# Merging two weight matrices as plain f32 products, in an attention and gated-layer kernel on one core

## The chip, the core and the metric

The kernel runs on one core of one Trainium2 chip. The metric is device time in microseconds (us); the times shown are of whole executions, and the profile is one execution recorded by the hardware.

## What is computed

The reference, cut to what matters (shapes: batch 4, 8 heads, 576 positions, head size 64; 2304 tokens of width 512):

```python
scores = scale * np.matmul(q, k.transpose(0, 1, 3, 2))
thresh = np.max(scores, axis=-1, keepdims=True) - tau
scores = np.where(scores >= thresh, scores, -1000000000.0)
...
x = attention output as [2304, 512]
x = (sigmoid(x @ w_gate) * (x @ w_val)) @ w_out        # d_ff 1536
a = x @ w1
b = x @ w2
h = a * b @ w3                                         # w3 is 1024 x 1024
out = h @ w_out2                                       # w_out2 is 1024 x 512
```

Weights arrive as 64-bit floats. Since `(a * b @ w3) @ w_out2` equals `(a * b) @ (w3 @ w_out2)`, the kernel forms the 1024 x 512 product `w3 @ w_out2` itself, once. This is the merge, and it is all that the change touches.

## The kernel before

**Stages.** Attention runs over 16 head pairs (4 batches of 4 pairs), each in 9 steps of 128 query rows, so 144 steps g (36 to a batch, 9 to a pair). A step's scores go into one of two PSUM buffers `ps_s` (`s_mm`, PE), then the row maximum (`s_max`, DVE, L321), the exponential and threshold (`s_exp`, ACT, L327 and L328), the mask into the tile `e` (`s_mask`, DVE, L336), a split of `e` into two f16 halves (`s_hi`, `s_lo`, ACT and POOL in batch 0), a DMA transpose into `pt` (`s_tr`, SP queue, L364), and 5 steps later the product with v (`pv`, PE, into `u`). The scores of step g+2 reuse the buffer of step g, so they wait for the mask of g. The first gated layer (`l1_gen`) of a batch runs beside the attention of the next batch, and that of the last batch after it; it can't begin before the attention of its batch is done (`ready`). The second layer and its output close the kernel (`ps_ab`, `ps_y`).

**A pair's inputs.** q and k are loaded, transposed on PE (`ps_t<-ident,qm` and `ps_t<-ident,km`, L156), split by ACT and DVE into a high and a low part, and copied by DMA into the stacked operands `qa`, `ka` (L206 to L210) and `ylz` (L216) of the scores. The table `ahead` (L826) says at which step of the pair before each of these pieces is issued.

**The merge.** `merge_gen` (L491) is a generator. `ucast` turns a loaded 128 x 512 block of 64-bit weights into f32: two DVE operations (L450, L456), one ACT (L455), one POOL (L459, tile `f`). There are 24 blocks: 8 of `w_out2` (`"o"`), 16 halves of the rows of `w3` (`"r"`). A block of `w_out2` is also split into a high part `woh` (ACT, L468) and a low part `wol` (DVE, L469). `trans` transposes half a row of `w3` with four PE transposes (L530), and splits the result from PSUM into `th` (ACT, L534) and `tl` (DVE, L535). For each of 8 rows, 8 products of 128 x 128 by 128 x 512 follow, each as three matmuls in the reduced format f32r (`three`, L471: high by low, low by high, high by high). The row's result is stored to DRAM as `sc_m` (L568) and is read again only in the last stage (L1114). All 12 first blocks are cast before the first product.

**What sets the order.** The attention loop calls `filler` (L838) twice in each step, which runs the merge for 700 ns of the generator's own prices (L841: `merge = run(merge, 700.0)`), and the first layer once the merge has ended. The scores, maxima, exponentials and masks are issued with a higher priority (L869). A scheduler then fixes the order of each engine's instructions by these priorities and by when it believes them ready, so the written place of a merge product isn't where it stands on PE. Each engine works its own list in order: an instruction that waits holds all behind it. All DMAs are issued from one list, that of SP.

Of the kernel before, what the change touches and what calls it, by code (L numbers as in the profile page):

```python
# [8 lines left out]
F32 = mybir.dt.float32  # L9
# [13 lines left out]
def kernel(  # L23
# [464 lines left out]
    def raw_slot(n):  # L488
        return XR[:, n % KC, 2 * S:2 * S + 2 * UW]

    def merge_gen():  # L491
        woh = mp.tile([P, NF2, DM], F32R, name="woh")
        wol = mp.tile([P, NF2, DM], F32R, name="wol")
        units = [("o", i, 0) for i in range(NF2)] + [("r", 0, 0), ("r", 0, 1)]
        units += [("r", i, h) for i in range(1, NF2) for h in range(2)]
        raws, rows, tr, done = {}, {}, {}, [0]

# [7 lines left out]
        def ucast():  # L505
            n = done[0]
            if n >= len(units):
                return
            done[0] += 1
            uload(n + 3)  # L510
            nm, i, h = units[n]
            t1 = mp.tile([P, UW], U32, tag="t1", name="t1", bufs=2)
            t2 = mp.tile([P, UW], I32, tag="t2", name="t2", bufs=2)
            f = mp.tile([P, UW], I32, tag="f", name="f", bufs=3)
            cast64(f, raws.pop(n), t1, t2)
            if nm == "o":
                split(woh[:, i], wol[:, i], f.bitcast(F32), nc.vector)
            else:
                rows[i, h] = f.bitcast(F32)

        def trans(i, h):
            if h == 0:
                tr[i] = tuple(
                    mp.tile([P, NF2, P], F32R, tag=g, name=g, bufs=2) for g in ("th", "tl")
                )
            th, tl = tr[i]
            r = rows.pop((i, h))
            ps = bank("ps_3")
            for j in range(4):
                nc.tensor.transpose(ps[:, j * P:(j + 1) * P], r[:, j * P:(j + 1) * P], ident)  # L530
            hs = slice(4 * h, 4 * h + 4)

            def out():
                nc.scalar.activation(th[:, hs].rearrange("p a b -> p (a b)"), ps, AF.Copy)  # L534
                nc.vector.tensor_tensor(  # L535
                    tl[:, hs].rearrange("p a b -> p (a b)"), ps,
                    th[:, hs].rearrange("p a b -> p (a b)").bitcast(F32), op=ALU.subtract,
                )

            defer.append(out)  # L540

        for n in range(3):
            uload(n)
        yield 0
        for i in range(NF2 + 4):
            ucast()
            yield 600.0
        trans(0, 0)
        trans(0, 1)
        yield 8 * 110  # L550
        flush(0)
        for i in range(NF2):
            th, tl = tr.pop(i)
            ps = bank("ps_34")
            for kk in range(NF2):
                three(
                    ps, (th[:, kk], tl[:, kk]), (woh[:, kk], wol[:, kk]),
                    kk == 0, kk == NF2 - 1,
                )
                if kk in (1, 4):  # L560
                    ucast()
                if kk in (2, 5) and i + 1 < NF2:
                    trans(i + 1, kk // 3)
                yield T(512, 3) + (4 * 110 if kk in (2, 5) else 0)
            def out(i=i, ps=ps):
                mo = mp.tile([P, DM], F32, tag="mo", name="mo", bufs=2)
                nc.scalar.activation(mo, ps, AF.Copy)
                nc.sync.dma_start(sc_m[i], mo)  # L568

            flush(0)  # L570
            defer.append(out)
        flush(0)


# [263 lines left out]
    def filler(g, half):  # L838
        nonlocal l1, merge, lp, lb
        if merge is not None:  # L840
            merge = run(merge, 700.0)  # L841
            if merge is None:
                mctx.close()
                spent[0] = 0
# [336 lines left out]
```

## Time and profile before

| | |
|---|---|
| Median of 3 executions | 1119.03 us (1117.58 to 1123.13) |
| Span of the profiled execution | 1115.6 us |
| Median less that span | 3.4 us |
| PE busy | 1008.3 us (90%) |
| DVE busy | 774.8 us (69%) |
| POOL busy | 676.3 us (61%) |
| ACT busy | 627.6 us (56%) |

The page gives the profiled execution's own time as its span; what lies around the span is not in it. Busy shares are averages over stages with different limits, so the stage in which the merge runs has to be read by itself: by its windows, by the order in which its steps start, and by what PE did in between. A matmul's record lasts longer than it holds PE, since matmuls are pipelined; how much PE time one costs is read from the distance of two starts.

### The profile page before, as it was taken

How to read it: one execution, taken by the hardware profiler on the slowest of the kernel's cores; microseconds unless marked ns; L12 is line 12 of the kernel's file. 1: busy time of each engine (PE TensorE's matmuls, PEld its weight loads, DVE VectorE, ACT ScalarE, POOL GpSimd, SP SyncE). 2: the span in 40 equal slices, each digit the busy share in tenths (PEclk: the TensorE clock that was granted, in tenths of full speed). 3: DMA queues.
4: the chain of work that ended last, by engine and by line, in shares of the span. 5: the costliest groups of instructions: out<-in, count | busy, mean ns of one | idle time of the engine just before them, and what ended most of it. 6: DMA issues, size and time to landing. Idle time of an engine off the chain costs nothing. (4 is left out here: it accounts for less than half of the span.)

```text
span 1115.6 us, 20323 instructions
## 1 busy us (share of the span) xinstructions
PE 1008.3 (90%) x6960; PEld 884.9 (79%) x6960; DVE 774.8 (69%) x1380; ACT 627.6 (56%) x1245; POOL 676.3 (61%) x577
## 2 busy tenths in 40 slices
PE   2598956898987999999999998999999999999997
PEld 2477845676765787777877888999999989988996
DVE  6978687888897767767877645776767644652741
ACT  4868898767777676567667644554442322331321
POOL 3755475587888586678677855677664643462530
PEclk9789967999988999999999999999999999999999
DMA  8999999999999999898988864677558826844922
GB/s 227 245 274 211 225 218 173 241 280 264 270 286 235 200 209 210 211 210 180 201 198 184 161 140 153 215 234 250 184 193 293 256 80 229 282 131 128 325 69 63
DMA packets 322422, 232.57 MB, mean 208 GB/s; under 512 B 225296, under 2 KB 253968, under 8 KB 322320
## 3 DMA queue, kind: packets, MB, share of 16 engines
q1 hardware_dynamic: 322320, 231.28, 80.9%
q8 instruction: 55, 0.90, 0.3%
q14 instruction: 47, 0.39, 0.1%
HBM read 133.17 MB, written 30.93 MB: 147 GB/s over the span
## 5 line engine op out<-in xcount | busy, mean ns | idle before, releaser
L358 POOL TENSOR_TENSOR h<-e,h 128x576 f16<-128x576 f32 x90 | 120.1, 1336 | 39.9 <-ACT e L355 29.7
L327 ACT ACTIVATE e<-ps_s,nm 128x576 f32<-128x576 f32 x144 | 106.1, 737 | 51.0 <-DVE nm L321 49.8
L336 DVE SCALAR_TENSOR_TENSOR e<-ps_s,th,e 128x576 f32<-128x576 f32 x144 | 116.2, 811 | 20.3 <-ACT th L328 12.5
L63 PEld LDWEIGHTS <-pt 128*128 128x128 f16 x2240 | 82.1, 101 | 58.8 <-DMA pt<-h 32.3
L321 DVE TENSOR_REDUCE nm<-ps_s 128x1 f32<-128x576 f32 x144 | 106.3, 751 | 28.9 <-PE ps_s L63 19.9
L344 ACT ACTIVATE h<-e 128x576 f16<-128x576 f32 x144 | 97.0, 678 | 28.3 <-DVE e L336 14.8
L63 PE MATMUL ps_s<-ka,qa 128*128 128x288 f32 x256 | 67.5, 351 | 42.2 <-DVE e L336 31.4
L63 PE MATMUL ps_h<-xl,gh 128*128 128x512 f32 (+1 forms) x240 | 94.7, 395 | 6.3 <-POOL xl L469 2.8
L63 PE MATMUL ps_h<-xl,vh 128*128 128x512 f32 (+1 forms) x240 | 92.7, 386 | 2.4 <-ACT th L685 1.3
L63 PE MATMUL ps_h<-xh,gl 128*128 128x512 f32 (+1 forms) x240 | 91.3, 380 | 3.3 <-POOL gl L469 3.3
L469 POOL TENSOR_TENSOR gl<-wg,gh 128x512 fp32r<-128x512 f32 x42 | 55.4, 1319 | 61.4 <-ACT gh L468 61.4
L63 PE MATMUL ps_y<-wm,abh 128*128 128x512 f32 x288 | 91.6, 390 | 0.2 <-DVE wm L469 0.2
L63 PE MATMUL ps_h<-xh,vl 128*128 128x512 f32 (+1 forms) x240 | 90.2, 376 | 1.6 <-POOL vl L469 1.6
L63 PE MATMUL ps_o<-gvl,oh 128*128 128x512 f32 (+1 forms) x240 | 90.4, 376 | 1.0 <-DVE XR L718 1.0
L63 PE MATMUL ps_h<-xh,gh 128*128 128x512 f32 (+1 forms) x240 | 90.8, 378 | 0.0
L63 PE MATMUL ps_h<-xh,vh 128*128 128x512 f32 (+1 forms) x240 | 90.2, 376 | 0.0
L63 PE MATMUL ps_o<-gvh,ol 128*128 128x512 f32 (+1 forms) x240 | 88.5, 369 | 0.3 <-POOL ol L469 0.3
L63 PE MATMUL ps_o<-gvh,oh 128*128 128x512 f32 (+1 forms) x240 | 88.2, 368 | 0.0
L63 PE MATMUL u<-vh,pt 128*128 128x64 f16 x640 | 62.6, 200 | 27.6 <-DMA pt<-h 27.2
L63 PEld LDWEIGHTS ps_s<-ka,qa 128*128 128x128 f32 x256 | 45.6, 210 | 50.5 <-DVE e L336 36.5
L360 DVE SCALAR_TENSOR_TENSOR h<-e,h 128x576 f16<-128x576 f32 x54 | 61.4, 1137 | 23.2 <-ACT h L344 22.8
L469 POOL TENSOR_TENSOR ol<-wo,oh 128x512 fp32r<-128x512 f32 x42 | 55.7, 1330 | 24.0 <-ACT oh L468 23.9
(198 smaller groups left out, 3025.2 us busy)
## 6 DMA issues: line engine op xcount, KB each, us to landing
wc<-sc_c SPq DMA_DIRECT2D x168, 256.0 KB, 3.2
sc_c<-wc SPq DMA_DIRECT2D x56, 256.0 KB, 2.9
XR<-in_moe_w_out_dram SPq DMA_DIRECT2D x20, 512.0 KB, 5.0
ka<-xk SPq DMA_DIRECT2D x64, 144.0 KB, 3.3
wg<-sc_g SPq DMA_DIRECT2D x36, 256.0 KB, 3.1
wv<-sc_v SPq DMA_DIRECT2D x36, 256.0 KB, 3.1
wo<-sc_o SPq DMA_DIRECT2D x36, 256.0 KB, 3.2
XR<-in_moe_w_dram SPq DMA_DIRECT2D x16, 512.0 KB, 5.0
```

What stands on the lines that cost most here:

```text
L63: nc.tensor.matmul(out_, lhsT, rhs, start=first, stop=last)
L321: nc.vector.tensor_reduce(nm, x["ps"], axis=AX.X, op=ALU.max, negate=True)
L327: nc.scalar.activation(e, x["ps"], AF.Exp, bias=x["nm"])
L336: nc.vector.scalar_tensor_tensor(x["e"], x["ps"], x["th"], x["e"], op0=ALU.is_ge, op1=ALU.mult, accum_out=prep[pr]["sum"][:, s:s + 1],)
L344: nc.scalar.activation(x["h16"][:, 0:S], x["e"], AF.Copy, scale=PSC)
L358: nc.gpsimd.tensor_tensor(lo, e, hi, op=ALU.subtract)
L360: nc.vector.scalar_tensor_tensor(lo, e, PSC, hi, op0=ALU.mult, op1=ALU.subtract)
L469: (lo_eng or nc.gpsimd).tensor_tensor(lo, x, hi.bitcast(F32), op=ALU.subtract)
```

## The change

The merge's products take unsplit f32 operands: one plain f32 matmul each (L564 of the changed kernel) instead of three f32r ones. `woh`, `wol`, `th` and `tl` go; `wo` and `wt` (one f32 tile each) stand in their place, the cast writes straight into `wo`, and `trans` leaves one ACT copy. The first half row of `w3` is cast first, then four blocks of `w_out2`, the other half, and the other four; the products of the first row begin after three casts and are issued between the rest. `filler` gives the merge, in each call, its remaining price divided by the calls that are left in batch 0.

```diff
+    CAST_NS = 600.0
+    MERGE_NS = NF2 * (NF2 * T(512, 4) + 8 * 110) + (NF2 + 4) * CAST_NS
+
     def merge_gen():
-        woh = mp.tile([P, NF2, DM], F32R, name="woh")
-        wol = mp.tile([P, NF2, DM], F32R, name="wol")
-        units = [("o", i, 0) for i in range(NF2)] + [("r", 0, 0), ("r", 0, 1)]
+        wo = mp.tile([P, NF2, DM], I32, name="wo")
+        units = [("r", 0, 0)] + [("o", i, 0) for i in range(NF2 // 2)]
+        units += [("r", 0, 1)] + [("o", i, 0) for i in range(NF2 // 2, NF2)]
         units += [("r", i, h) for i in range(1, NF2) for h in range(2)]
...
-            f = mp.tile([P, UW], I32, tag="f", name="f", bufs=3)
-            cast64(f, raws.pop(n), t1, t2)
             if nm == "o":
-                split(woh[:, i], wol[:, i], f.bitcast(F32), nc.vector)
+                cast64(wo[:, i], raws.pop(n), t1, t2)
             else:
+                f = mp.tile([P, UW], I32, tag="f", name="f", bufs=4)
+                cast64(f, raws.pop(n), t1, t2)
                 rows[i, h] = f.bitcast(F32)
...
-            def out():
-                nc.scalar.activation(th[:, hs].rearrange("p a b -> p (a b)"), ps, AF.Copy)
-                nc.vector.tensor_tensor(
-                    tl[:, hs].rearrange("p a b -> p (a b)"), ps,
-                    th[:, hs].rearrange("p a b -> p (a b)").bitcast(F32), op=ALU.subtract,
+            defer.append(
+                lambda: nc.scalar.activation(
+                    t[:, hs].rearrange("p a b -> p (a b)"), ps, AF.Copy
                 )
-
-            defer.append(out)
+            )
...
-        for i in range(NF2 + 4):
+        for n in range(3):
             ucast()
-            yield 600.0
+            yield CAST_NS
         trans(0, 0)
-        trans(0, 1)
-        yield 8 * 110
+        yield 4 * 110
...
             for kk in range(NF2):
-                three(
-                    ps, (th[:, kk], tl[:, kk]), (woh[:, kk], wol[:, kk]),
-                    kk == 0, kk == NF2 - 1,
-                )
-                if kk in (1, 4):
+                ns = T(512, 4)
+                if i == 0:
+                    for _ in range(2 if kk == 6 else 1):
+                        ucast()
+                        ns += CAST_NS
+                    if kk == 4:
+                        flush(0)
+                    if kk == 3:
+                        trans(0, 1)
+                        ns += 4 * 110
+                elif kk in (1, 4):
                     ucast()
+                mm(ps, t[:, kk], wo[:, kk].bitcast(F32), kk == 0, kk == NF2 - 1)
...
-            merge = run(merge, 700.0)
+            merge = run(merge, (MERGE_NS - spent[0]) / max(2 * (NPAIR * NSL - g) - half, 1))
```

**Where PE transposes the keys of the second pair.** These are rows of PE in the first pair (g 0 to 8). `km` is the loaded k, `ps_s_88` and `ps_s_89` are the score buffers of even and odd steps, `ylz_96` an operand of the scores of the pair's second head, `pt` and `u` belong to the product with v. Before:

```order
L63 LDWEIGHTS pt
L63 MATMUL u<-vsh,pt 128x64
L156 MATMUL ps_t<-ident,km 128x128 x4
L63 LDWEIGHTS pt
L63 MATMUL u<-vh,pt 128x64
```

Changed:

```order
L63 MATMUL ps_s_89<-identb,vm 128x128
L531 MATMUL ps_383<-ident,f 128x128 x4
L63 MATMUL ps_s_88<-ka,qa 128x288 x2
L63 MATMUL ps_s_88<-ylz_96,qa 128x288 x2
L156 MATMUL ps_t<-ident,km 128x128 x4
L63 LDWEIGHTS pt
L63 MATMUL u<-vh,pt 128x64
```

Before, the transposes of `km` stand behind the scores of g 8 and six steps' products with v; in the change they stand right behind the scores of g 6, ahead of those of g 7 and of all but one step's products with v.

**Where PE takes the first scores of the second pair** (g 9 and 10). `woh`, `wol`, `th`, `tl`, `wo` and `wt` are the merge's operands, `xk`, `yk` and `qbd_90` those of the scores of g 8. Before:

```order
L63 MATMUL ps_483<-woh,th 128x512
L63 MATMUL ps_483<-wol,th 128x512
L530 MATMUL ps_524<-ident,f 128x128 x4
L63 MATMUL ps_483<-woh,tl 128x512
L63 MATMUL ps_483<-woh,th 128x512
L63 MATMUL ps_s_89<-ka,qa 128x288 x2
L63 MATMUL ps_s_88<-ka,qa 128x288 x2
L63 MATMUL ps_s_89<-ylz_95,qa 128x288 x2
L63 MATMUL ps_s_88<-ylz_95,qa 128x288 x2
L530 MATMUL ps_575<-ident,f 128x128 x4
L63 MATMUL ps_625<-wol,th 128x512
```

Changed:

```order
L63 MATMUL ps_s_88<-xk,qbd_90 128x288 x4
L63 MATMUL ps_s_88<-yk,qbd_90 128x288 x2
L63 MATMUL ps_314<-wo,wt 128x512
L63 LDWEIGHTS vb
L63 MATMUL ps_s_89<-identb,vb 128x128
L63 MATMUL ps_314<-wo,wt 128x512
L531 MATMUL ps_513<-ident,f 128x128 x4
L63 MATMUL ps_s_89<-ka,qa 128x288 x2
L63 MATMUL ps_s_89<-ylz_95,qa 128x288 x2
L63 MATMUL ps_s_88<-ka,qa 128x288 x2
L63 MATMUL ps_s_88<-ylz_95,qa 128x288 x2
L531 MATMUL ps_527<-ident,f 128x128 x4
L63 MATMUL ps_546<-wo,wt 128x512 x8
```

Before, all 24 f32r matmuls of the merge's first row (22 of them in front of the rows shown first, two between the transposes and the scores) stand between the scores of g 8 and those of g 9. In the change only the last two of the first row's eight plain products do, and the second row's eight stand behind the scores of g 10.

**Where SP issues the fourth transpose into `pt`** (g 3; `h_510` before, `h_447` in the change). `XR` holds the raw weight blocks, `sc_m_136` is the merge's first row in DRAM. Before:

```order
L206 DMA qa<-xq 64x512
L207 DMA qa<-yq 64x512
L206 DMA qa<-xq 64x512
L207 DMA qa<-yq 64x512
L440 DMA XR<-in_moe_w_dram 128x512
L149 DMA tails<-in_k_dram 64x2x64
L364 DMA_TRANSPOSE pt<-h_510 128x9x128
```

Changed:

```order
L206 DMA qa<-xq 64x512
L207 DMA qa<-yq 64x512
L440 DMA XR<-in_moe_w_dram 128x512
L210 DMA ka<-xk 64x576 x2
L573 DMA sc_m_136<-mo 128x512
L145 DMA km<-in_k_dram 128x4x64 x2
L149 DMA tails<-in_k_dram 64x2x64
L440 DMA XR<-in_moe_w_dram 128x512
L364 DMA_TRANSPOSE pt<-h_447 128x9x128
```

Before, it waits behind two blocks and the query copies; in the change also behind the key copies of the second pair and the store of the merge's first row, which needs that row's eight products.

## Rows read from the trace of the kernel before

**Rows 1.** The page: span, and PE's granted clock in 40 slices.

```profile
span 1115.6 us, 20323 instructions
...
PEclk9789967999988999999999999999999999999999
```

**Rows 2.** The chain that ended last, its first steps (start us, us, what).

```profile
672.66 0.31 ACT XR L420
...
674.70 10.19 PE ps_h L63 x48
```

**Rows 3.** Windows: length, busy PE, PEld, DVE, ACT, POOL (instructions), clock, DMA share, GB/s.

```profile
0.00:25.00 25.00, 7.17 (x28) 5.71 (x28) 14.88 (x37) 10.02 (x18) 5.67 (x14) 1.00 0.84 206
25.00:50.00 25.00, 10.05 (x70) 8.05 (x70) 24.60 (x49) 21.48 (x43) 19.05 (x15) 0.89 1.12 257
...
75.00:100.00 25.00, 22.66 (x211) 19.55 (x209) 21.45 (x44) 21.33 (x43) 14.41 (x12) 1.00 1.08 242
100.00:125.00 25.00, 23.06 (x194) 19.67 (x193) 19.26 (x37) 20.57 (x42) 13.72 (x12) 1.00 0.90 211
125.00:150.00 25.00, 20.04 (x191) 16.97 (x189) 15.69 (x36) 19.33 (x37) 9.33 (x9) 0.93 0.91 217
```

**Rows 4.** DVE in order of time: masks of g 7, 9, 27, 29, 33.

```profile
51.48 0.81 DVE L336 SCALAR_TENSOR_TENSOR e<-ps_s,th,e 128x576 f32<-128x576 f32 x1
...
72.08 0.80 DVE L336 SCALAR_TENSOR_TENSOR e<-ps_s,th,e 128x576 f32<-128x576 f32 x1
...
147.38 0.81 DVE L336 SCALAR_TENSOR_TENSOR e<-ps_s,th,e 128x576 f32<-128x576 f32 x1
...
155.83 0.82 DVE L336 SCALAR_TENSOR_TENSOR e<-ps_s,th,e 128x576 f32<-128x576 f32 x1
...
167.95 0.80 DVE L336 SCALAR_TENSOR_TENSOR e<-ps_s,th,e 128x576 f32<-128x576 f32 x1
```

**Rows 5.** PE in order of time: scores of g 6 and 8, product with v, keys, scores of g 9.

```profile
39.21 0.83 PE L63 MATMUL ps_s<-ka,qa 128*128 128x288 f32 x2
...
46.21 0.68 PE L63 MATMUL ps_s<-yk,qbd 128*128 128x288 f32 x2
...
51.30 0.24 PE L63 MATMUL u<-vh,pt 128*128 128x64 f16 x1 [3.01 <-DMA pt<-h]
...
56.02 1.10 PE L156 MATMUL ps_t<-ident,km 128*128 128x128 f32 x4
...
67.96 0.70 PE L63 MATMUL ps_s<-ka,qa 128*128 128x288 f32 x4
```

**Rows 6.** PE in order of time: first-row matmuls of the merge at the lower clock.

```profile
61.72 0.63 PE L63 MATMUL ps<-woh,th 128*128 128x512 f32 x1
62.15 0.63 PE L63 MATMUL ps<-wol,th 128*128 128x512 f32 x1
```

**Rows 7.** PE in order of time: one transpose, four, first and sixth merge matmul.

```profile
75.96 0.27 PE L165 MATMUL ps_s<-ident,tails 128*128 128x128 f32 x1
...
76.59 0.60 PE L530 MATMUL ps<-ident,f 128*128 128x128 f32 x4
...
78.42 0.40 PE L63 MATMUL ps<-wol,th 128*128 128x512 f32 x1
...
79.57 0.39 PE L63 MATMUL ps<-woh,th 128*128 128x512 f32 x1
```

**Rows 8.** The tile woh: weight load ahead of a merge matmul, min/median/max ns.

```profile
L63 PEld LDWEIGHTS ps<-woh,th x64: 187/188/330, 60.0 to 138.8; 128*128 128x128 f32 x64
```

**Rows 9.** Groups in 0 to 205 us: the splits that go.

```profile
L535 DVE TENSOR_TENSOR tl<-ps,th 128x512 fp32r<-128x512 f32 x16 | 11.0, 686 | 6.3 <-ACT th L534 6.3
...
L469 DVE TENSOR_TENSOR wol<-f,woh 128x512 fp32r<-128x512 f32 x8 | 6.1, 756 | 0.0
...
L468 ACT ACTIVATE woh<-f 128x512 fp32r<-128x512 f32 x8 | 5.0, 622 | 4.6 <-POOL f L459 4.6
```

More of the change, by code (lines that the diff above doesn't have):

```diff
@@ L522, in trans @@
             if h == 0:
-                tr[i] = tuple(
-                    mp.tile([P, NF2, P], F32R, tag=g, name=g, bufs=2) for g in ("th", "tl")
-                )
-            th, tl = tr[i]
+                tr[i] = mp.tile([P, NF2, P], F32, tag="wt", name="wt", bufs=2)
+            t = tr[i]
             r = rows.pop((i, h))
@@ L544, in merge_gen @@
         yield 0
-        for i in range(NF2 + 4):
+        for n in range(3):
             ucast()
-            yield 600.0
+            yield CAST_NS
         trans(0, 0)
-        trans(0, 1)
-        yield 8 * 110
+        yield 4 * 110
         flush(0)
         for i in range(NF2):
-            th, tl = tr.pop(i)
+            t = tr[i]
             ps = bank("ps_34")
             for kk in range(NF2):
-                three(
-                    ps, (th[:, kk], tl[:, kk]), (woh[:, kk], wol[:, kk]),
-                    kk == 0, kk == NF2 - 1,
-                )
-                if kk in (1, 4):
+                ns = T(512, 4)
[9 more added lines that the diff above has]
+                elif kk in (1, 4):
                     ucast()
-                if kk in (2, 5) and i + 1 < NF2:
+                mm(ps, t[:, kk], wo[:, kk].bitcast(F32), kk == 0, kk == NF2 - 1)
+                if i and kk in (2, 5) and i + 1 < NF2:
                     trans(i + 1, kk // 3)
-                yield T(512, 3) + (4 * 110 if kk in (2, 5) else 0)
+                    ns += 4 * 110
+                yield ns
             def out(i=i, ps=ps):
@@ L570, in merge_gen @@
             flush(0)
+            tr.pop(i)
             defer.append(out)
+            if i == 0:
+                for h in range(2):
+                    trans(1, h)
+                    ucast()
+                yield 8 * 110
+                flush(0)
         flush(0)
```

## The prediction

> **What bounds the kernel now.** I read four views, from the end backwards. The page gives a span of 1115.6 us [rows 1]. The median of the runs is 1119.0, so 3.4 us lie around the span; the sum below is made against the span, and 3.4 is added at the end. The chain that ended last goes back to the last transposed attention output at 672.66 and to the layer's matmuls that wait for it at 674.70 [rows 2]; behind that point PE works almost without a gap, and the change touches nothing there. So the change counts only by how much earlier or later the attention gets through. The merge lies wholly inside batch 0. Nothing of the first layer's matmuls can begin until that batch's attention is done, so an us won or lost in batch 0 moves all that follows by about an us.
>
> In batch 0 the windows show two different states [rows 3]. Up to 50 us PE is busy 7.17 and 10.05 of each 25 us: it waits. From 75 to 150 us it is busy 22.66 + 23.06 + 20.04 = 65.8 of 75 us, with 9.2 us idle, while DVE is busy 56.4 of the 75: there PE is the fullest engine, and the merge is what fills it. The masks on DVE mark the pace of the attention. With no merge, g 29 to g 33 take 167.95 - 155.83 = 12.1 us, so two steps take 6.1 [rows 4]. That is the pace of the chain score, maximum, exponential, mask. From g 7 to g 9 two steps take 72.08 - 51.48 = 20.6 us [rows 4]. This stall of 14.5 us is the largest single loss of batch 0.
>
> PE in order of time says what stood in the way [rows 5]. The scores of g 8 end near 46.9. Then products with v wait for their DMA transposes (3.01 us idle before 51.30, one of several), and because PE takes its list in order, the transposes of the second pair's keys behind them begin only at 56.02. The scores of g 9, which need those keys, begin at 67.96, which is 11.9 us later; in between lie the splits, the key copies by DMA, and 24 merge matmuls, the first of them at half the clock.
>
> **The price of a product.** At the higher clock six merge matmuls start in 79.57 - 78.42 = 1.15 us, five distances of 0.23 [rows 7]; three make a product of 0.69 us. At the lower clock the distance is 62.15 - 61.72 = 0.43 [rows 6]. The trace has no plain f32 product, so I bound it. Below: a single f32 transpose of 128 columns is recorded with 0.27 us and four with 0.60 [rows 7], so one more costs (0.60 - 0.27) / 3 = 0.11; four such stretches make 512 columns, 0.44 us. Above: four passes of 0.23, each with a weight load of 0.19 [rows 8] that nothing hides: 1.68 us. I take 4 x 0.23 = 0.92: an f32 number is a high and a low part, a product of two such has four partial products, and the kernel now leaves one of the four out at 0.23 each. The change's own planner has the same factor of 4 to 3. This lies between the ends, and nearer the matmul row than the transposes, which multiply nothing. The Trainium skill, "FP8 and Floating Point Precision", section TensorE Precision Notes, has a rule that speaks against the transposes' rate and so against a cheaper product: true FP32 takes four passes through the array. By that rule a product is an estimated 0.92 us and the sum is the one below; by the transposes' row alone it would be 0.44 us and the third rival below. No run so far shows which.
>
> **The change part by part.**
>
> *Keys of the second pair earlier: -14.0 us.* In the changed order these transposes follow the scores of g 6, which began at 39.21 and end by about 40.3 [rows 5]. With the same 11.9 us from keys to scores, g 9 can begin at 52.2, which is also when the mask of g 7, 0.81 us from 51.48, frees its buffer [rows 4]. From scores to mask took 72.08 - 67.96 = 4.1 us. Two plain products still stand in front, 1.8 us. So the mask of g 9 comes at 58.1 in place of 72.08. Between zero, if something else holds g 9, and 14.5.
>
> *First row of products moved into g 0 to 8: +1.7 us.* Eight products, at half the clock 4 x 0.43 = 1.7 us each. One stands between the two halves of the very first scores and delays them: +1.7. Two are counted above. The other five, 8.6 us, fall where PE idles 15 of 25 us [rows 3]; that idle time hides them. If the cover is gone, +8.6.
>
> *The other 56 products: +5.5 us.* Each is dearer by 0.92 - 0.69 = 0.23, together 12.9 us of PE. They stand in the same stretch as before: in the order of PE the last eight come before the scores of g 27, so the even spreading that `filler` asks for does not reach the engine, since the scheduler takes a product when it is ready. If all of PE's 9.2 us idle there took them, 3.7 us would be left; if none, 12.9. I take 5.5, nearer the lower end, because over half of the idle time (5.0 us) lies in the last 25 us [rows 3], where the change's last products go.
>
> *Splits removed: -2.0 us.* Of 16 subtractions `tl` at 0.686 us, 14 lie behind g 9, 9.6 us of DVE [rows 9]. DVE has 18.6 us idle in the stretch [rows 3], so most were hidden; I take a fifth, with ends of 0 and -9.6. The 8 `wol` (6.1 us) and 8 `woh` (5.0 us) lie before 50 us, where PE waits for DMA transposes: 0, with -5 as the other end. If something replaced them as the late operand, it would be the casts, which stay.
>
> *Casts in another order: 0.* The same 24 loads, casts, and DMAs. SP's list now has the store of the first row, and the key copies, ahead of the transpose of g 3. That transpose waits for eight products, and SP holds all behind it. Who waits is the product with v of g 3, which in the changed order stands behind the scores of g 12; so nothing that sets the pace. If it did, one period, +6.1.
>
> *First layer's opening casts: 0.* They ran beside g 27 to 29, whose two steps took 155.83 - 147.38 = 8.5 us [rows 4], 2.4 over the pace. Now the merge ends later by `filler`'s count and they move to about g 34 to 38, still before the layer may begin. They should cost the same 2.4 there; ends -2.4 and +2.4.
>
> Sum: -14.0 + 1.7 + 5.5 - 2.0 = -8.8. Span 1106.8, and with 3.4 around it 1110.2 us. Faster and slower are counted from 0.5%, 5.6 us, about what a measurement of this kernel can tell from no change.
>
> **The rivals.**
>
> *The rows of eight give the stall back: no change.* The products stand in rows of eight in front of scores; eight last 7.4 us in place of 5.5, and a period of 6.1 us has room for far less beside its own matmuls. If each of the seven rows behind g 9 passes its 1.8 us on whole, +12.9, and the removed splits give nothing: -14.0 + 1.7 + 12.9 = +0.6, 1119.6 us. For it: PE is at 88% there. Against it: the 9.2 us idle. Chance 0.28.
>
> *The plain product is dear: slower.* If its weight loads are not hidden, 1.68 us each, the 56 products cost 56 x 0.99 = 55.4 more, less 7.4 hidden as above: -14.0 + 1.7 - 2.0 + 48.0 = +33.7, 1152.7 us. Its place is the same stretch, 72 to 147 us before. It decides from a price of about 1.18 us: there 56 x 0.49 - 7.4 - 14.3 makes the +5.6. For it: f32 operands are read in more than one piece. Against it: the weight loads of the f32r matmuls (0.19) hide under a pass of 0.23. Chance 0.12.
>
> *The plain product is cheap: much faster.* At the transposes' 0.44, the 56 products save 14.0 us of PE, of which 88% on the path, 12.3: -14.0 + 1.7 - 2.0 - 12.3 = -26.6, 1092.4 us. Against it: a transpose only copies. Chance 0.08.
>
> **How the numbers follow.** The forecast has 0.52: 1110.2 us. Its own ends, by the stretch's bounds of 3.7 to 12.9 and the first row's cover, are 1103 to 1113. Faster is the forecast and the cheap product, 0.60; the same is the first rival, 0.28; slower the second, 0.12. The range of 1095 to 1123 holds the forecast and the first rival with a few us of scatter and part of the cheap product; it leaves out the dear product and the rest.
>
> **What would show it.** The masks of g 7 and g 9 stand some 7 us apart in place of 20.6, with the second pair's keys transposed near 40 us; if they stand 15 or more apart, the first step is wrong. The distance of two plain products at the higher clock is 0.92 us; 0.44 or over 1.18 makes the forecast wrong. The mask of g 27 comes near 138 to 141 us in place of 147.4; if it comes at 147, the rows of eight gave the stall back. The first layer's matmuls begin about 9 us earlier, and the chain's 672.66 becomes about 664. What would make the forecast wrong with each step right is batches 1 to 3, where the scheduler's list also changes a little: I count nothing for it.

## The result, and the profile after

The changed kernel takes 1124.54 us (median of 16 runs, 1121.13 to 1128.16), the kernel before 1118.44 us (16 runs, 1115.09 to 1125.07): a ratio of 1.0051, 95% interval 1.0034 to 1.0067. The forecast was 1110.2 us, in a range of 1095 to 1123. The kernel became slower by about the least that counted as slower. The profiled span went from 1115.6 [rows 1] to 1124.7 us, 9.1 us more. The medians differ by 6.1 us only: the changed kernel's profiled execution took 1126.71 us, 2.2 above its median. It also shows that some 2.0 us lie around a span, not the 3.4 of the prediction's sum.

The page of the changed kernel, the same two lines as in [rows 1]:

```profile
span 1124.7 us, 20189 instructions
...
PEclk9889896989989899999999999999999999999999
```

The chain that ended last, its first steps, to be held against [rows 2]:

```profile
681.49 1.01 POOL xl L469
682.55 10.16 PE ps_h L63 x48
```

These matmuls began at 674.70 before and begin at 682.55: 7.9 of the 9.1 us are there at that point. So most of the loss was made before, in the attention. Where batch 0 ends is best seen on PE: the first layer's first matmul stands at 190.29 us before and at 199.97 us after, 9.7 us later.

Windows cut at two places, the mask of g 9 (72.1 before, 60.0 after) and this first matmul, answer to [rows 3]. The columns are those of [rows 3]. Of the kernel before:

```profile
0.00:72.10 72.10, 35.95 (x218) 29.45 (x219) 56.27 (x114) 44.58 (x84) 37.00 (x38) 0.86 1.01 243
72.10:190.30 118.20, 92.58 (x833) 79.10 (x831) 93.80 (x191) 97.87 (x195) 68.90 (x57) 0.87 0.99 217
```

Of the changed kernel:

```profile
0.00:60.00 60.00, 30.71 (x147) 20.04 (x148) 44.19 (x95) 34.79 (x68) 29.31 (x34) 0.91 0.89 228
60.00:200.00 140.00, 108.20 (x834) 73.88 (x832) 90.27 (x179) 101.47 (x200) 73.03 (x62) 0.86 0.99 208
```

This is the main reading. Up to the first layer PE is busy 35.95 + 92.58 = 128.5 us before and 30.71 + 108.20 = 138.9 after: 10.4 us more. It is idle 190.3 - 128.5 = 61.8 us before and 200.0 - 138.9 = 61.1 after: the same. The two stretches can be compared, since they hold nearly the same other work: 1051 matmuls less the merge's 192 are 859 before, 981 less 128 are 853 after. Up to g 9 the idle time fell from 36.2 to 29.3 us, and behind g 9 it grew from 25.6 to 31.8 us. The change took a wait away, and waits of the same sum came back; what was left is the work added.

DVE in order of time, masks of g 7, 9, 11 and 27 (before: 51.48, 72.08 and 147.38 in [rows 4], and 82.0 for g 11):

```profile
54.63 0.81 DVE L336 SCALAR_TENSOR_TENSOR e<-ps_s,th,e 128x576 f32<-128x576 f32 x1
...
60.01 0.80 DVE L336 SCALAR_TENSOR_TENSOR e<-ps_s,th,e 128x576 f32<-128x576 f32 x1
...
79.99 0.82 DVE L336 SCALAR_TENSOR_TENSOR e<-ps_s,th,e 128x576 f32<-128x576 f32 x1
...
157.16 0.81 DVE L336 SCALAR_TENSOR_TENSOR e<-ps_s,th,e 128x576 f32<-128x576 f32 x1
```

The stall between g 7 and g 9 is gone: 5.4 us in place of 20.6. But g 9 to g 11 take 20.0 us in place of 9.9, and at g 27 the kernel is 9.8 us behind.

The next view shows one of those who held g 11. SP's list in order of time, around the fourth transpose into `pt` (g 3); POOL had finished the half that it needs at 43.6 us:

```profile
42.70 1.81 SPq L364 DMA_TRANSPOSE pt<-h  x1
...
53.33 2.32 SPq L210 DMA_DIRECT2D ka<-xk  x2
55.94 0.35 SPq L573 DMA_DIRECT2D sc_m<-mo  x1
56.59 2.32 SPq L145 DMA_DIRECT2D km<-in_k_dram  x2
...
61.59 1.82 SPq L364 DMA_TRANSPOSE pt<-h  x1
```

The transpose was ready at 43.6 and was issued at 61.59, 18.0 us later, behind key copies and the first merged row's store. Before, the delay was 5.7 us. ACT in order of time (start, us, ..., idle time before it and its releaser in brackets) shows who waited for it:

```profile
66.44 0.68 ACT L344 ACTIVATE h<-e 128x576 f16<-128x576 f32 x1 [4.11 <-DMA pt<-h]
...
77.68 0.73 ACT L327 ACTIVATE e<-ps_s,nm 128x576 f32<-128x576 f32 x1
```

The halves `h` have four buffers, so the half of g 7 waits until the transpose of g 3 has read its own. It stands in ACT's list ahead of the exponential of g 11 (77.68), behind which the mask comes at 79.99.

ACT was not the only one that held g 11. Its scores were done on PE at 66.0, but DVE took their maximum only at 74.93, behind casts of weights, some of which waited for their loads (1.95 us for the first shown). DVE in order of time:

```profile
65.50 0.70 DVE L450 TENSOR_SCALAR ps_c<-XR 128x512 uint32<-128x512 uint32 x1 [1.95 <-DMA XR<-in_moe_w_dram]
...
74.93 1.41 DVE L321 TENSOR_REDUCE nm<-ps_s 128x1 f32<-128x576 f32 x2
```

How much of the 20.0 us is the transpose's, a run has to say (a_tr3 below).

The product itself. PE in order of time, then its group over the whole span (busy, mean ns of one, idle before):

```profile
58.03 7.03 PE L63 MATMUL ps<-wo,wt 128*128 128x512 f32 x16
```

```profile
L63 PE MATMUL ps<-wo,wt 128*128 128x512 f32 x128 | 64.8, 649 | 1.9 <-POOL wo L459 1.9
```

Sixty-four products are 128 records, so a plain product is recorded as two. Sixteen of them take 7.03 us from the first start to the last end; the last record lasts 0.59, so the distance is (7.03 - 0.59) / 15 = 0.43 us, and a product holds PE for 0.86 us. The price taken was 0.92, against 0.69 for the three f32r matmuls [rows 7]. Sixty-four products are then 0.17 x 64 = 10.9 us dearer, which is nearly the 10.4 us found in the windows.

### The profile page after: what moved, and what is told of

Same layout as the page of the kernel before. It is cut to its first block, busy times and chain, and to the rows that moved or that the text cites. A ratio compares the mean times of both kernels' runs of the same rounds, so it can differ in the third digit from the quotient of the medians.

```text
span 1124.7 us, 20189 instructions
## 1 busy us (share of the span) xinstructions
PE 1021.5 (91%) x6896; PEld 873.4 (78%) x6896; DVE 762.2 (68%) x1356; ACT 621.2 (55%) x1237; POOL 673.6 (60%) x577
## 5 line engine op out<-in xcount | busy, mean ns | idle before, releaser
L469 POOL TENSOR_TENSOR ol<-wo,oh 128x512 fp32r<-128x512 f32 x42 | 55.6, 1325 | 26.1 <-ACT oh L468 25.6
```

Source lines behind the costliest of these rows:

```text
L469: (lo_eng or nc.gpsimd).tensor_tensor(lo, x, hi.bitcast(F32), op=ALU.subtract)
```

## The experiments

Each run was timed against the kernel before, in five rounds, on one chip with it; a ratio is that to the kernel before. "First layer" is the start of its first matmul (before 190.3, after 200.0). Three theories were in play: **work** (PE's dearer products make the loss), **list** (transposes held in SP's list), **opening** (the even spread ends the merge later, so the first layer's opening loads and casts come late).

The runs were made in four series: the first four of the table, the next four, then a_tr3_again, a_split_tr3, b_two and b_four, then a_two, a_split_tr30 and a_tr3_lo; the result above is a series of its own. The same kernel in two series (a_tr3 and a_tr3_again) gave 1.0108 and 1.0056, with intervals that don't meet. So between series a difference of half a percent is less sure than the intervals say. "First layer" and "span" are of one execution each.

| Run | what it is | median us | ratio, 95% interval | first layer | span |
|---|---|---|---|---|---|
| a_split | after, three split products | 1116.68 | 0.9987, 0.9976 to 0.9998 | 192.3 | 1117.2 |
| b_plain | before, plain products | 1119.28 | 1.0016, 1.0003 to 1.0029 | 196.0 | 1119.7 |
| a_rate | after, 700 ns per call | 1121.08 | 1.0031, 1.0016 to 1.0046 | 195.3 | 1124.8 |
| a_trprio | after, all transposes first | 1131.80 | 1.0121, 1.0101 to 1.0140 | 199.2 | 1130.6 |
| a_split_rate | a_split, 700 ns per call | 1120.39 | 1.0032, 1.0016 to 1.0049 | 195.0 | 1119.4 |
| a_early | after, spread up to g 24 | 1127.79 | 1.0108, 1.0089 to 1.0127 | 203.0 | 1128.7 |
| b_even | before, even spread | 1124.54 | 1.0067, 1.0045 to 1.0088 | 194.3 | 1121.1 |
| a_tr3 | after, transpose of g 3 first | 1128.07 | 1.0108, 1.0087 to 1.0129 | 192.0 | 1121.5 |
| a_tr3_again | the same | 1123.90 | 1.0056, 1.0035 to 1.0077 | 191.8 | 1121.7 |
| a_split_tr3 | a_split, transpose of g 3 first | 1119.61 | 1.0024, 1.0002 to 1.0045 | 195.8 | 1117.2 |
| b_two | before, two split products | 1117.65 | 1.0000, 0.9983 to 1.0017 | 197.6 | 1117.0 |
| b_four | before, four split products | 1132.01 | 1.0124, 1.0099 to 1.0149 | 206.6 | 1131.6 |
| a_two | a_split, two of three products | 1117.92 | 1.0001, 0.9983 to 1.0019 | 194.3 | 1116.0 |
| a_split_tr30 | a_split, late transposes first | 1127.61 | 1.0077, 1.0048 to 1.0106 | 189.6 | 1127.5 |
| a_tr3_lo | a_tr3, one VectorE step moved | 1117.04 | 1.0001, 0.9975 to 1.0026 | 190.0 | 1111.3 |

### The products alone

a_split puts the split operands and the three f32r matmuls back into the changed order; b_plain puts the plain matmul into the order before. Of a_split:

```diff
...
-                mm(ps, t[:, kk], wo[:, kk].bitcast(F32), kk == 0, kk == NF2 - 1)
+                three(
+                    ps, (th[:, kk], tl[:, kk]), (woh[:, kk], wol[:, kk]),
+                    kk == 0, kk == NF2 - 1,
+                )
...
```

> The changed kernel with the three f32r products per product put back (splits of both operands too); cast order and even spread as changed. If the dearer plain product is what costs (0.86 us on PE against 0.69, 56 of them behind g 9, 9.6 us), this comes out some 6 to 10 us faster than the changed kernel, at or below before (1115 to 1119). If SP's list is what costs, it depends on where the transposes into pt stand there: in this one's list the fourth still stands behind the key copies but ahead of the first row's store, so g 9 to g 11 should take clearly under the 20.0 us of the changed kernel. If the late opening casts of the first layer cost, g 36 to g 43 stays near 29 us and the time stays within 3 us of the changed kernel.

> The kernel before with plain f32 products alone; cast order and 700 ns a call as before. If the dearer product costs, 4 to 10 us slower than before (1122 to 1128). If SP's list or the late first layer costs, both come with the other parts of the change, and this one is within 3 us of before.

With the split products the changed order costs nothing (0.9987); with the plain ones 0.51%. The difference of the two ratios, 0.0064, is 7.2 us. That is not the price of the product alone, for the order moved with it. SP's list of a_split has the fourth transpose 5.5 us earlier than the changed kernel's:

```profile
56.10 4.52 SPq L364 DMA_TRANSPOSE pt<-h  x2
```

Its g 9 to g 11 take 8.3 us and not 20.0, as was expected if SP's list costs. Two runs of one series in both of which this transpose stands first, a_tr3_again and a_split_tr3, differ by 0.0032, 3.6 us, and a part of that is a slow DVE instruction that only the first of them has (below). So the plain product by itself costs at most 7.2 us in this order; how much less was not measured apart. a_split also shows the other half of the answer: with the dear product undone, all the rest of the change, the removed stall among it, is worth 0.13%, 1.4 us. In the order before the plain product cost only 0.16%, 1.8 us, less than the work theory expected; there it moved the second pair forward too (mask of g 9 at 64.7 against 72.1), so its own price cannot be read from that run.

### PE's work more and less, in the order of before

b_two leaves a product out, b_four adds one (low by low); nothing else is edited:

```diff
-                three(
-                    ps, (th[:, kk], tl[:, kk]), (woh[:, kk], wol[:, kk]),
-                    kk == 0, kk == NF2 - 1,
-                )
+                mm(ps, th[:, kk], wol[:, kk], kk == 0, False)
+                mm(ps, th[:, kk], woh[:, kk], False, kk == NF2 - 1)
```

```diff
+                mm(ps, tl[:, kk], wol[:, kk], kk == 0, False)
                 three(
                     ps, (th[:, kk], tl[:, kk]), (woh[:, kk], wol[:, kk]),
-                    kk == 0, kk == NF2 - 1,
+                    False, kk == NF2 - 1,
                 )
```

> The kernel before with two of the three split products in the merge (the product of the low half of w3 with the high half of w_out2 is left out: 64 matmuls of 0.23 us, 14.7 us of TensorE, the yields left as they are). Theory that TensorE's work in batch 0 sets the time: the matmuls' busy time up to the first layer falls by 13 to 16 us from 128.5, its idle time there stays near 62, first ps_h at 174 to 181 us, the whole 1102 to 1109 us. Theory that waits (transposes in SP's list, casts that wait for loads) set it and TensorE's work fits beside them: idle grows by what the work falls, first ps_h 186 to 191, whole 1114 to 1119.

> The kernel before with a fourth split product in the merge (low half by low half added: 64 matmuls of 0.23 us, 14.7 us more of TensorE, a product at 0.92 us, the price the forecast had taken for the plain one). TensorE theory: busy time up to the first layer 141 to 145, idle near 62, first ps_h at 201 to 206 us, whole 1127 to 1133. Theory of waits: part of it goes into the idle time, first ps_h 192 to 198, whole 1119 to 1125.

The two give different verdicts. Windows of b_four, cut at its mask of g 9 and its first layer:

```profile
0.00:71.70 71.70, 36.16 (x225) 29.86 (x226) 56.84 (x115) 44.35 (x85) 36.86 (x38) 0.88 1.00 246
71.70:206.60 134.90, 106.41 (x885) 89.84 (x883) 93.98 (x188) 98.93 (x195) 68.48 (x57) 0.85 0.88 194
```

and of b_two:

```profile
0.00:73.40 73.40, 34.67 (x212) 28.32 (x213) 56.12 (x113) 44.69 (x84) 36.92 (x38) 1.00 0.97 237
73.40:197.60 124.20, 92.49 (x825) 77.37 (x823) 98.06 (x203) 101.51 (x205) 70.22 (x58) 0.78 0.97 211
```

With 14.7 us of PE work more, busy time to the first layer is 142.6 us, 14.1 more than before; idle 64.0; the whole is 13.9 us longer (1.24%). With 14.7 us less the whole is the same. Idle rises to 70.4 us, and busy time falls by only 1.4 us to 127.2. But b_two's first layer is not the same mark as before: 1037 matmuls stand ahead of it, where 1051 - 64 = 987 would; the attention of batch 0 is done there in both, so some 50 matmuls of the next batch have moved in front of it. The whole times count here. They are one-sided: the PE work that b_four adds was paid in full, that which b_two takes away was not paid back. A change that trades a stall for PE work stands on the wrong side of that.

### Both taken away

a_two makes b_two's edit in a_split, so both the stall and the work are gone.

> The changed order and spread with two of three split products (the low half of w3 by the high half of w_out2 left out): the stall ahead of the second pair is gone as in the run of 1116.7 us with three, and 14.7 us of TensorE's work besides. In the kernel before, taking the same work away alone gave nothing (1.0000), and taking the stall away alone gave nothing to speak of (0.9987). Theory of two limits side by side, where each alone is covered by the other: both together give 6 to 12 us, first ps_h at 178 to 186 us, whole 1104 to 1111. Theory that a third limit (SP's list, the first layer's opening) holds the first layer whatever TensorE does: first ps_h at 189 to 196, whole 1113 to 1119.

The whole has a ratio of 1.0001, as was expected for a third limit. Here the first layer is a like mark. Windows of a_split:

```profile
0.00:65.10 65.10, 33.70 (x174) 26.21 (x174) 52.66 (x103) 39.49 (x76) 30.87 (x34) 0.76 0.93 228
65.10:192.30 127.20, 99.54 (x909) 82.59 (x908) 101.75 (x207) 103.18 (x208) 76.08 (x62) 0.87 1.00 221
```

and of a_two:

```profile
0.00:65.50 65.50, 29.80 (x166) 22.03 (x167) 52.50 (x104) 39.75 (x77) 31.45 (x35) 0.90 0.94 230
65.50:194.30 128.80, 92.40 (x852) 77.90 (x851) 102.96 (x208) 102.33 (x206) 74.78 (x61) 0.80 0.99 219
```

They differ by 65 matmuls, the 64 left out and one. Busy time falls from 133.2 to 122.2 us, idle time rises from 59.1 to 72.1: waits took all the room that the work left. The two limits do not simply cover each other. Which is the third stays open; its place is behind the masks of batch 0, for a_two's mask of g 36 stands 11.0 us ahead of before (168.19 against 179.24) and that of g 54 4.6 us behind (255.92 against 251.30).

### The transpose that SP's list held

a_trprio places every transpose into `pt` with priority; a_tr3 only that of g 3:

```diff
-        if 2 <= g < G + 2:
+        if g == 5:
+            with tc.high_priority(offset=RING):
+                s_tr(g - 2)
+        elif 2 <= g < G + 2:
             s_tr(g - 2)
```

> The changed kernel with the transposes into pt issued at the priority of the scores, which puts the fourth to sixth ahead of the key copies and of the first row's store in SP's list. If SP's list took the win back, the wait of ACT for the transpose of g 3 (4.1 us) goes, g 9 and g 11 no longer stand 20 us apart, the mask of g 11 comes 6 to 10 us earlier than 79.8, and the time falls by 5 to 10 us, to 1114 to 1120. If the casts on DVE that wait for their loads hold g 11, its mask stays at 76 to 82 us, and the time changes by under 3 us.

> The changed kernel with one edit: the fourth transpose into pt (step 3) is placed with priority, so that it stands in SP's list right behind the third and ahead of the copies of the second pair's queries and keys, the store of the first merged row and the loads of keys. Theory of the held transpose: ACT's wait for the ring of halves at step 7 (4.1 us) goes, the masks of steps 9 to 11 lie 14 to 17 us apart in place of 20.0, mask of step 11 at 75 to 78 us, first ps_h 195 to 198, whole 1119 to 1122. Theory that the price of the products alone matters, the wait being covered: mask of step 11 within 2 us of 80.0, whole 1123 to 1126. The key copies behind it come later by the 3 us for which the transpose waits, so that the scores of step 9 may come up to 3 us later in both.

a_trprio missed: masks g 9 to g 11 came to 11.4 us, but g 9 itself came at 66.6, and with all 144 steps changed more was lost later. a_tr3 is the clean one, and half a miss: the mask of g 11 came at 74.6 us (75 to 78 expected), the first layer at 192.0, 8.0 us earlier than after, and PE's idle time up to it fell from 61.1 to 54.3 us. So the held transpose did cost 8 us at the first layer. The whole gained nothing (1128.07, and 1123.90 in the second series, where 1119 to 1122 was expected). The trace shows the place, 55 us later. DVE of a_tr3:

```profile
246.50 7.09 DVE L360 SCALAR_TENSOR_TENSOR h<-e,h 128x576 f16<-128x576 f32 x1
253.52 1.27 DVE L730 TENSOR_SCALAR XR<-ps_o 128x512 f32<-128x512 f32 x2
```

POOL of a_tr3:

```profile
246.78 1.29 POOL L459 TENSOR_TENSOR wo<-t,t 128x512 int32<-128x512 int32 x1
248.03 1.28 POOL L469 TENSOR_TENSOR vl<-wv,vh 128x512 fp32r<-128x512 f32 x1
249.28 1.25 POOL L459 TENSOR_TENSOR wg<-t,t 128x512 int32<-128x512 int32 x1
250.50 1.26 POOL L469 TENSOR_TENSOR ol<-wo,oh 128x512 fp32r<-128x512 f32 x1
251.72 1.25 POOL L469 TENSOR_TENSOR gl<-wg,gh 128x512 fp32r<-128x512 f32 x1
```

and PE of a_tr3:

```profile
254.25 0.80 PE L63 MATMUL ps_h<-xl,gh 128*128 128x512 f32 x1 [4.89 <-DVE XR L730]
```

The low half of g 51 took 7.09 us where its like take 1.2, beside POOL instructions without a gap, and ended 0.6 us behind the last of them. PE stood for 4.89 us for the DVE operation behind it. The next runs ask whether that was chance, and what it costs; a_tr3_lo computes this one half on POOL:

```diff
-        if b == 0 or g % 2 == 0:
+        if b == 0 or g % 2 == 0 or g == 51:
```

> The same kernel as the one before with the fourth transpose into pt placed with priority, again, for its profile: there the first layer began 8 us earlier than in the changed kernel, and the lead was gone 60 us later, at one instruction of VectorE that took 7.1 us (246.5 us, the rest of the form 1.2) beside six of GpSimd. If that was a chance of the one execution: no instruction of that form above 4 us, first ps_h again at 191 to 194, span 1114 to 1118. If the order itself makes it: again one of 6 to 8 us near 246 us, span 1120 to 1128.

> The changed kernel with the fourth transpose placed with priority, and the low half of step 51 computed on GpSimd (with its scaling on ScalarE, as for even steps) and not on VectorE, where it took 7.1 us in both profiles beside GpSimd instructions without a gap, against 1.2 for its like. If that one instruction loses the lead of 8 us that the first layer had: no VectorE instruction of the form above 4 us near 246, TensorE's idle time between first ps_h and the first quarter of the first layer falls from 30.0 to 24 to 26 us, whole 1116 to 1120. If the lead is lost to the pace of the first layer's loads and casts whatever this instruction does: idle there 28 to 31 us, whole 1122 to 1128.

It was no chance: 7.10 us at 245.6 in the second execution, span 1121.7. a_trprio has one too, 6.26 us at 188.97, again ending 0.6 us behind a row of POOL instructions without a gap. With the half of g 51 moved (a_tr3_lo), no instruction of the form lasts over 3.1 us. The masks of g 51 to 53 of a_tr3 stand 0.2 to 2.0 us behind those of a_tr3_lo, that of g 54 stands 9.5 us behind. Mask of g 54, first of a_tr3, then of a_tr3_lo:

```profile
261.69 0.82 DVE L336 SCALAR_TENSOR_TENSOR e<-ps_s,th,e 128x576 f32<-128x576 f32 x1 [0.86 <-ACT th L328]
...
252.18 0.82 DVE L336 SCALAR_TENSOR_TENSOR e<-ps_s,th,e 128x576 f32<-128x576 f32 x1 [0.83 <-ACT th L328]
```

The windows from the first layer's start to its first quarter, first of a_tr3:

```profile
192.00:412.70 220.70, 190.69 (x1505) 156.73 (x1503) 185.75 (x333) 155.38 (x310) 156.99 (x128) 0.92 1.02 242
```

then of a_tr3_lo:

```profile
190.00:405.30 215.30, 190.68 (x1503) 156.58 (x1502) 179.23 (x334) 157.98 (x312) 159.02 (x129) 0.92 1.06 248
```

PE's work is the same, 190.7 us; the stretch is 5.4 us shorter, its idle time 24.6 in place of 30.0 us. The whole is 1117.04 us, a ratio of 1.0001; the execution in the trace is the fastest of twelve (1113.07 to 1124.03). Two small edits of the order bring the kernel back to the time of before with the plain products kept; the gain over the changed kernel, 0.5%, is as large as the scatter between series, so its size is less sure than the wait that went. What the second edit alone would do, for the kernel before or for the changed one, was not tried. Of all runs only a_split is below the kernel before with its whole interval, by 0.13%.

### The spread and the first layer's opening

a_rate and a_split_rate give the merge 700 ns per call again; a_early aims the even spread at g 24; b_even brings the even spread into the kernel before. Of a_early:

```diff
-            merge = run(merge, (MERGE_NS - spent[0]) / max(2 * (NPAIR * NSL - g) - half, 1))
+            merge = run(merge, (MERGE_NS - spent[0]) / max(2 * (24 - g) - half, 1))
```

> The changed kernel with 700 ns a call put back; plain products and cast order as changed. If the first layer's late opening casts cost (g 36 to g 43 28.9 us against 21.7), that stretch comes back to 22 to 24 us and the time falls by 4 to 7 us. If SP's list in the first pair costs, nothing changes there: the first row's store still stands ahead of the fourth transpose, g 9 to g 11 stays near 20 us, and the time stays at 1121 to 1125.

> The changed kernel with three products of split operands put back (as the run before that had 1116.7 us) and, besides, the merge's time given out at 700 ns per call as before, so that the merge ends sooner and the first layer's opening loads are asked for earlier. Theory that the late opening of the first layer costs time: in the split kernel the masks were 8 us ahead of before at step 36 and the first layer's first matmul still 2 us behind, because its opening loads at 164 to 174 us stand in SP's list ahead of the transposes of steps 30 to 33; with the opening some 30 us earlier the lead should reach the first layer: first ps_h at 184 to 189 us (before 190.3, split 192.3) and the whole 1110 to 1114 us. Rival, that the opening is only where a loss made elsewhere shows: the early steps are spread less thinly, the lead of 8 us shrinks, first ps_h at 190 to 193, whole 1115 to 1119.

> The changed kernel with its even spread aimed at step 24 of batch 0 and not at step 36, plain products kept: the late opening is taken away, the dearer products are not. Late-opening theory: first ps_h at 194 to 197 us (after: 200.0), whole 1118 to 1121. If only the price of the products (about 0.17 us more on each of 64, on a TensorE that sets the pace of batch 0) makes the loss, nothing is gained: first ps_h 198 to 201, whole 1123 to 1126, since the same work stands in fewer steps.

> The kernel before with nothing changed but that the merge's time is given out evenly over the 36 steps (three products of split operands, casts in the order of before). Late-opening theory: the steps up to 20 go faster than before, the first layer opens near step 35 and loses it again and more: first ps_h 192 to 196 us, whole 1119 to 1124. If the even spread is harmless or good by itself: first ps_h 186 to 190, whole 1112 to 1118.

b_even had its first layer as expected (194.3) and its whole just above the range: the even spread alone costs 0.67% in the order before. But a_early and a_split_rate missed, in the same direction: aimed at an earlier end, the changed kernel read slower (1.0108, though a_tr3 read the same in that series), and so did a_split (1.0032). In a_early the steps g 9 to g 18 take 62.9 us in place of 54.8, with PE busy 54.0 of them: the dear products stand closer. So the spread was a loss in one order and none in the other, and its price doesn't add to the others. a_rate (1.0031, its interval meets that of the changed kernel) is no clean test of the opening: a product's price in the generator is 905 ns, so a call of 700 ns runs one product, and the merge ends nearly as late as with the even spread (148.8 against 153.3 us).

a_split had its masks 8.2 us ahead of before at g 36, and its first layer 2.0 us behind. SP's list of a_split shows transposes behind the opening loads; that of g 30, whose half was ready at 155.0, is the first:

```profile
163.80 0.59 SPq L440 DMA_DIRECT2D XR<-in_moe_w_gate_dram  x1
164.44 0.51 SPq L440 DMA_DIRECT2D XR<-in_moe_w_val_dram  x1
164.99 1.06 SPq L440 DMA_DIRECT2D XR<-in_moe_w_gate_dram  x2
166.14 4.30 SPq L364 DMA_TRANSPOSE pt<-h  x1
```

a_split_tr30 places the transposes of g 28 to 35 with priority (the edit of a_tr3 with `30 <= g < 38`), and a_split_tr3 the one of g 3.

> The changed order with three split products and the transposes of steps 28 to 35 placed with priority, so that those of steps 30 to 33 stand in SP's list ahead of the first layer's opening loads of w_gate and w_val, behind which they waited 11 to 17 us. Theory that the lead of 8 us at step 36 was lost at these transposes: first ps_h at 183 to 187 us (192.3 without the edit), whole 1108 to 1113. Rival, that the opening loads and casts, late themselves (163 to 178 us), set the first layer's begin: they come later still, first ps_h 191 to 197, whole 1115 to 1121.

> The changed order with three split products (the run that had 1116.7 us) and, besides, the fourth transpose into pt placed with priority ahead of the copies of queries and keys. If the two losses add (TensorE's work by the plain product; idle time of TensorE by the held transpose, 6.8 us less in the changed kernel's first 200 us with the same edit): first ps_h at 183 to 187 us, idle up to it 52 to 55, whole 1108 to 1114. If the wait in SP's list is only pushed on to the transposes of steps 30 to 33, which stand behind the first layer's opening loads: first ps_h 190 to 193, whole 1115 to 1120.

Both missed. In a_split_tr30 the first layer began 2.7 us earlier, with fewer matmuls of the next batch ahead of it, but its loads came 6 us later and PE's idle time to the first quarter rose from 25.5 to 33.6 us: 1.0077. A transpose moved forward in SP's list moves a load backward that is needed as well. In a_split_tr3 the first layer came 3.5 us later. The gain of a_tr3 belongs to the plain product's order and does not carry over.

## Why the prediction was wrong

The forecast missed by 1124.5 - 1110.2 = 14.3 us. a_split, which has all of the change but the plain product and the removed splits, parts the miss in two. All but these was forecast at -14.0 + 1.7 = -12.3 and measured -1.4, 10.9 us off. The product and the splits were forecast at 5.5 - 2.0 = +3.5 and measured at most 7.2, 3.7 off. By its own steps:

- **Keys of the second pair earlier, -14.0: this step failed.** Its mechanism held. Keys were transposed at 44.09 (near 40 forecast), the masks of g 7 and g 9 stand 5.4 us apart (7 forecast), and g 9 came 12.1 us earlier. But the worth of it failed: a_split, with the dear product taken out, is 7.0 us ahead at g 9 and 8.2 at g 36, and gains 1.4 us. The sum took a lead at one mask for a lead at the end of the kernel. Other waits came in the stall's place: PE is idle for 61.1 us up to the first layer where it was 61.8. One of them is known, the held transpose (next step). What takes the lead of a_split and a_two behind g 36 stays open.
- **Casts in another order, 0: failed, and by a stated bound.** "Who waits is the product with v of g 3 ... so nothing that sets the pace" overlooked the ring of four halves: ACT's half of g 7 waits for the same transpose. The other end, +6.1, was near: a_tr3 measured 8.0 us at the first layer.
- **First row of products, +1.7: too small.** The mask of g 0 came 3.9 us later (25.10 against 21.24), that of g 7 3.2. The product between the two halves of the first scores cost what was forecast; the rest is that these scores began 2.1 us later, behind transposes of `w3` that wait for their cast, and at the end for the copy of `ka`. PE of the kernel before, then of the changed one:

```profile
17.68 1.30 PE L63 MATMUL ps_s<-ka,qa 128*128 128x288 f32 x4 [9.32 <-DVE t L456]
...
16.91 1.12 PE L531 MATMUL ps<-ident,f 128*128 128x128 f32 x4 [8.21 <-POOL f L459]
...
19.83 1.30 PE L63 MATMUL ps_s<-ka,qa 128*128 128x288 f32 x4 [1.81 <-DMA ka<-xk]
```

- **The other 56 products, +5.5, and the price:** 0.86 us against 0.92 taken. The idle time was to hide over half of it; PE's busy time shows 10.4 us more up to the first layer, idle time unchanged, so nothing was hidden up to there. The whole pays at most 7.2 us; the bounds were 3.7 to 12.9. The Trainium skill, "FP8 and Floating Point Precision", section TensorE Precision Notes, which gives true FP32 four passes, is borne out by the size, 0.86 being close to 4 x 0.23; the trace shows two records and not four.
- **Splits removed, -2.0:** not tried alone; it is part of the 7.2 us, which are net of it.
- **First layer's opening, 0 with ends of 2.4:** the opening loads of `w_gate` and `w_val` went from 120 us to 141 and 174 us, and the even spread alone cost 0.67% in the order before. In the changed order the spread was no loss (a_split_rate, a_early). What it costs in the changed kernel stays open.
- **"An us won or lost in batch 0 moves all that follows by about an us":** half right. b_four lost 16.3 us at the first layer and 16.0 at the end of its span. a_tr3 won 8.0 us against the changed kernel and 3.2 at the end, since a wait behind the first layer took the rest. b_two's 7.3 us at the first layer and 1.4 at the end say little, since it had more of the next batch done by then.
- **The forecast's own ends, 1103 to 1113:** they don't follow from the bounds they name. With 12.9 us for the 56 products in place of 5.5 the sum is 1117.6, and with the first row uncovered, 8.6 us more, 1126.2. Added up, the stated ends reach the measured time.

Of the rivals, the first ("rows of eight give the stall back", 1119.6) is nearest in kind: the mask of g 27 came at 157.2, far behind the 147 named as its sign. It had +0.6 in place of the measured 6.1 and left out the held transpose. The dear and the cheap product are excluded by 0.86 us. The chance of slower was tied to the dear product alone; no rival had a wait in SP's list that takes the place of the one removed, though the order showed it and a bound had been worked out for it.

## What to carry to other kernels

Before a removed stall is credited with its length, add up the idle time of the same engine over the whole stage to the point where the next stage starts; if the other waits there lie ready behind it, the sum stays and only the work added or taken counts. A transpose or store that waits in a single DMA list is to be followed to every user of its source buffer, not only to the reader of its result: here it was the ring of halves that passed the wait on. Where PE waits as well as works, price its work from both sides: in the order of before 14.7 us more cost 13.9 us and 14.7 us less gave nothing. A mark such as the first matmul of the next stage is to be compared only where the same work stands ahead of it.

## What the runs showed of the hardware that was not expected

A DVE instruction with two operands in SBUF, the on-chip memory of the engines, took 7.09 us (a_tr3) and 7.10 (a_tr3_again) in place of 1.2, in a_tr3 beside five POOL instructions that followed each other without a gap from 246.78 to 252.97 us, after a sixth that was under way. A third, in a_trprio, took 6.26 us and ended 0.6 us behind such a row as well. The Trainium skill, "SBUF — State Buffer", section Who interferes with whom, says that such a DVE instruction contends with a GpSimd (POOL) instruction that reads SBUF, and that the ports they share are an exclusive lock. The trace agrees that it is held up; it was held here for the whole row and not for one instruction of 1.28 us.

A plain f32 product of 128 x 128 by 128 x 512 is recorded as two matmuls, whose starts lie 0.43 us apart (58.03 to 65.06 us), 0.86 us for the product, where one f32r matmul of this size takes 0.23 [rows 7].
